# Output blocks of one tile by seven half-width products instead of eight, their operand sums on GpSimd

## The chip, the cores and the metric

One core of a Trainium2 chip runs the whole kernel. The metric is the device time of one execution in microseconds (us). TensorE (PE) multiplies matrices into PSUM banks; VectorE (DVE), ScalarE (ACT) and GpSimd (POOL) do element-wise work; SyncE (SP) issues the transfers (DMA). Each engine works through its own queue in order.

## The reference

A recurrent attention with a decay per head, then a feed-forward layer that multiplies two projections element by element:

```
for t in range(S):                                  # B, H, S, D = 4, 8, 768, 64
    state = gamma * state + k[:, :, t] (outer) v[:, :, t]
    y[:, :, t] = scale * q[:, :, t] @ state
x = y as (B*S, H*D) = (3072, 512)
a = x @ w_a;  b = x @ w_b                           # d_ff = 1536
return (a * b @ w_out)                              # (3072, 512), float32
```

## The kernel before

The 3072 tokens are 24 slots of 128. Seven tiles take them in turn: `TILES = [4, 2, 2, 2, 2, 4, 8]` (line 16), so tile 0 is slots 0 to 3, tile 1 is slots 4 and 5, tile 2 slots 6 and 7. A program written out by hand (lines 887 to 1068) fixes the order of each engine's instructions: `seq` (line 94) chains every instruction behind the one before it on the same engine, and between engines only data and buffers make one wait.

Around the change the program does these things.

- `casts_two(t)` and `casts(t)` (lines 304 and 287) prepare slots: GpSimd scales k and q into `kqb` (line 280) and copies v into `vb` (line 239), SP issues the DMA transpose of `kqb` into `kqT` (`flip`, line 300) and then the loads of a later slot. All of this goes into the queues of GpSimd and SP at the place of the call.
- `turn(new, old)` (line 389) does the attention of a pair of slots: `update` (TensorE into the state bank `st`, then a cast to `gst` by ScalarE or by the engine given), `scores` (TensorE into two banks, then two DVE multiplications by the mask into `aT`, line 333) for the new pair; `inter`, `intra` (TensorE into the banks `y0`, `y1`) and `leave` (ScalarE) for the old pair.
- `ffn_ab(J, ft)` computes one of the 12 column blocks of a*b for tile J: four matmuls for a, a ScalarE copy, four for g, a DVE multiplication into `ht` (lines 522 to 536).
- `ffn_out(J, i, n)` (line 553) is half n of the plain output block i of tile J: six matmuls of 512 columns. Both halves make one block of 128 rows; ScalarE copies it out, and the store is put on SP's queue by the next `store()`.
- `Group(J, i, A, B, C)` (line 617) makes two output blocks at once in the Strassen-Winograd manner, by seven products `p1` to `p7` of six matmuls of 256 columns each, in three PSUM banks A, B and C. `p2` ends with a DVE addition that reads bank C, after which C goes back to the ring; `p7` takes bank B; `p4` and `p5` end with DVE additions that read bank B; `p1`, `p6`, `p5` are followed by ScalarE snapshots of bank A, `p3` by a ScalarE copy.
- The products need sums of operands. `weight_sum(3)`, `(2)`, `(1)`, `(4)` (line 576) make T3, T2, T1 and T4 out of the output weights, each in two DVE halves of 768 elements a partition; they are made once and used by every tile. `hsum(J, s, a, b, eng)` (line 596) makes sum s of tile J out of `ht`: sum 3 is read by `p7`, 2 by `p6`, 1 by `p5`, 4 by `p3`. `hsums` makes 2, 1 and 4. T3 is read by `p7`, T2 by `p6`, T1 by `p5`, T4 by `p4`.
- The ring `psff` (line 69) hands out the three banks `ff0` to `ff2` in the order in which they were given back. `hs_tile` (line 588) says out of which pool a tile's sums come: `wstage`, which has six buffers under the tag `w`, or `raw`.

In the version before, the four output blocks of tile 0 are all made by `ffn_out`, and tiles 1 and up use `Group`. The branch for tile 0 in `hs_tile` is not reached.

Of the kernel before, what the change touches and what calls it, by code (L numbers as in the profile page):

```python
# [10 lines left out]
BF16 = mybir.dt.bfloat16  # L11
# [12 lines left out]
def kernel(  # L24
# [11 lines left out]
    P = 128  # L36
# [19 lines left out]
    wstage = ctx.enter_context(tc.tile_pool(name="wstage", bufs=6))  # L56
    raw = ctx.enter_context(tc.tile_pool(name="raw", bufs=3))
    nat = ctx.enter_context(tc.tile_pool(name="nat", bufs=6))
    tra = ctx.enter_context(tc.tile_pool(name="tra", bufs=4))
# [45 lines left out]
    def load_slot(t, names="kqv"):  # L105
        b, ci = divmod(t, NCH)
        for nm in names:
            src = {"k": k, "q": q, "v": v}[nm]
            if nm == "q":
                if t % 2 == 0:  # L110
                    load_two(nm, src, b, ci // 2, t)
                continue
            if t % 2 == 0:
                whole[nm] = raw.tile([P, 2, H, D], F32, tag=nm + "f", name=nm + "f")
            raws[nm, t] = whole[nm][:, t % 2]
            s = src[b, :, ci * P : (ci + 1) * P, :].rearrange("h p d -> p h d")
            seq(nc.sync.dma_start(out=raws[nm, t], in_=s))
# [108 lines left out]
    NP = NFT // 2  # L226
# [5 lines left out]
    BIG = len(TILES) - 1  # L232
    NS = NP - 1

    def cast(engine, dst, src):
        if engine is nc.scalar:
            seq(nc.scalar.copy(dst, src))
        else:
            seq(engine.tensor_copy(dst, src))  # L239
# [19 lines left out]
    kb, qb, vb, kqT, aT = {}, {}, {}, {}, {}  # L259
# [9 lines left out]
    def scaled(eng, t, i):  # L269
        tab = tabs[0] if i else tabs[1 if t < 2 * PAIRS else 2]  # L270
        dst, src, tab = kqb[t][:, i], raws["kq"[i], t], tab[:, t % NCH]
        if t < 2 * PAIRS:
            dst, src = (x.rearrange("p (hp r) d -> p hp r d", r=2) if x is src else x
                        for x in (dst, src))
            tab = tab.rearrange("p (hp r) o -> p hp r o", r=2).to_broadcast([P, HP, 2, D])
        else:
            dst = dst.rearrange("p hp r d -> p r hp d")
            src = src.rearrange("p (r hp) d -> p r hp d", r=2)
            tab = tab.rearrange("p (r hp) o -> p r hp o", r=2).to_broadcast([P, 2, HP, D])
        seq(eng.tensor_tensor(dst, src, tab, op=ALU.mult))  # L280

    def new_nat(t):
        kqb[t] = nat.tile([P, 2, HP, 2, D], BF16, tag="kqb", name="kqb")
        kb[t], qb[t] = kqb[t][:, 0], kqb[t][:, 1]
        vb[t] = nat.tile([P, H, D], BF16, tag="vb", name="vb")

    def casts(t):
        new_nat(t)
        scaled(nc.gpsimd, t, 0)
        scaled(nc.gpsimd, t, 1)  # L290
        if t not in range(12, 20):
            cast(nc.gpsimd, vb[t], raws["v", t])
        flip(t)
        if t + 2 < NSLOT:
            load_slot(t + 2)

    def flip(t):
        if t % 2 == 0:
            kqT[t // 2] = tra.tile([P, 2, 2, HP, P], BF16, tag="kqT", name="kqT", bufs=3)
        seq(nc.sync.dma_start_transpose(  # L300
            out=kqT[t // 2][:, t % 2].rearrange("p a b c -> p (a b) c"),
            in_=kqb[t].rearrange("p a hp r d -> p (a hp r d)")))
# [67 lines left out]
    def intra(t):  # L370
        for r in range(2):
            for j in range(2):
                for c in range(2):
                    hp = 2 * j + c
                    seq(nc.tensor.matmul(ys[t // 2][r][half(c), j, :, t % 2, :],  # L375
                                         vb[t][:, HP * r + hp, :], aT[t][:, r, hp, :],
                                         start=begin(t, c, r), stop=True, skip_group_check=True))
# [11 lines left out]
    def turn(new, old, eng=nc.scalar):  # L389
        if old is not None:  # L390
            ys[old // 2] = [psat.tile([P, 2, 2, 2, P // 2], F32, tag=f"y{r}", name="y") for r in range(2)]
        two = new is not None and (new + 1) % NCH < NCH - 1
        if new is not None:
            if two or old is None:
                update(new, eng)
            scores(new + 1, "y" if old is None else "ff")
            scores(new, "at")
        if old is not None:
            inter(old)
            inter(old + 1)  # L400
        if two:
            update(new + 1, nc.scalar)
        elif new is not None and old is not None:
            update(new, eng)
        if old is not None:
            intra(old)
            intra(old + 1)
            leave(old)
# [144 lines left out]
    def ffn_out(J, i, n):  # L553
        if n == 0:
            store()
            plain_out[i] = psff.tile([P, DM], F32, tag="ff", name="o")
        o = plain_out[i]
        for ft in range(NP * n, NP * n + NP):
            seq(nc.tensor.matmul(o, ht[J][:, ft, i * P : (i + 1) * P], wo_bf[:, ft],  # L559
                                 start=(ft == 0), stop=(ft == NFT - 1), skip_group_check=True))  # L560
        if n:
            osb = osbp.tile([P, DM], F32, tag="osb", name="osb")
            cast(nc.scalar, osb, o)
            psff.back(o)
            held.append((rows(J, i // 2, i % 2), osb))
# [5 lines left out]
    def tt(dst, x, y, op, eng=nc.vector):  # L571
        seq(eng.tensor_tensor(dst, x, y, op=op))  # L572
# [3 lines left out]
    def weight_sum(n, halves=(0, 1)):  # L576
        if n == 1 and not T1:
            T1.append(wstage.tile([P, NP, DH], BF16, tag="w", name="wsum1"))
        x, y, op = {3: (B22, B12, ALU.subtract), 2: (T3, B11, ALU.add), 4: (B21, T2, ALU.subtract),
                    1: (B12, B11, ALU.subtract)}[n]  # L580
        dst = T1[0] if n == 1 else {2: T2, 3: T3, 4: T4}[n]
        for i in halves:
            j = slice(NP // 2 * i, NP // 2 * (i + 1))
            tt(dst[:, j], x[:, j], y[:, j], op)

    hs = {}

    def hs_tile(J, s):
        if (J, s) not in hs:
            pool, tag = (raw, ("kf", "qf", "vf", "kf")[s - 1]) if J in (0, (BIG, 1)) else (wstage, "w")  # L590
            bufs = {}
            if (J, s) == (0, 4):
                pool, tag, bufs = tra, "kqT", {"bufs": 3}
            hs[J, s] = pool.tile([P, NP, 2, P], BF16, tag=tag, name=f"hs{s}", **bufs)

    def hsum(J, s, a, b, eng=nc.vector):
        U = slice(int(J == 0), 2 if isinstance(J, tuple) else TILES[J] // 2)
        hs_tile(J, s)
        v = ht[J].rearrange("p (k j) (u r n) -> p r k j u n", k=2, r=2, n=P)
        A11, A12, A21, A22 = (v[:, r, k2, a:b, U] for r in range(2) for k2 in range(2))  # L600
        S = {x: hs[J, x][:, a:b, U] for x in (1, 2, 3, 4) if (J, x) in hs}
        x, y, op = {3: (A11, A21, ALU.subtract), 2: (A22, S[3], ALU.subtract), 1: (A21, A22, ALU.add),
                    4: (A12, S.get(2), ALU.subtract)}[s]
        tt(S[s], x, y, op, eng)

    def hsums(J, a, b, eng):
        for s in (2, 1, 4):
            hsum(J, s, a, b, eng)
# [94 lines left out]
    FF = (psff, "ff")  # L703
# [3 lines left out]
    def single(J, A, B, C):  # L707
        g = Group(J, 0, A, B, C)
        g.p1()
        g.p7()  # L710
        g.p2()
        ffn_ab(J + 1, 0)
        g.p6()
        ffn_ab(J + 1, 1)
        g.p5()
        ffn_ab(J + 1, 2)
        g.p3()
        g.p4()
# [166 lines left out]
    D_, G_, A_ = nc.vector, nc.gpsimd, nc.scalar  # L885
# [72 lines left out]
    V_ = nc.vector  # L958
# [7 lines left out]
    def three(J, ft):  # L966
        store()
        for f in range(ft, ft + 3):
            ffn_a(J, f)
        for f in range(ft, ft + 3):  # L970
            ffn_g(J, f)
# [4 lines left out]
    for ft in range(NFT):  # L976
        ffn_ab(1, ft)
    casts_two(6)
    ffn_out(0, 0, 0)
    weight_sum(3)  # L980
    weight_sum(2)
    ffn_out(0, 0, 1)
    weight_sum(1)
    ffn_out(0, 1, 0)
    ffn_out(0, 1, 1)
    weight_sum(4)
    casts(8)
    ffn_out(0, 2, 0)
    ffn_out(0, 2, 1)
    turn(6, None, V_)  # L990
    hsum(1, 3, 0, 6)
    hsums(1, 0, 6, V_)
    ffn_out(0, 3, 0)
    ffn_out(0, 3, 1)
    casts(9)
    turn(None, 6)
    single(1, AT0, AT1, FF)
    casts(10)
    casts(11)
# [1 line left out]
    hsum(2, 3, 0, 6, G_)  # L1001
    blocks(2, 6, 7)
    turn(8, None)
    three(2, 7)
    hsums(2, 0, 3, G_)
    casts(12)
    turn(None, 8)
    blocks(2, 10, NFT)
    hsums(2, 3, 6, G_)
# [3 lines left out]
    blocks(3, 3, 4)  # L1013
    turn(10, None, V_)
    three(3, 4)
    hsum(3, 3, 0, 6, G_)
    v_cast(12)
    blocks(3, 7, 8)
    v_cast(13)
    blocks(3, 8, 9)  # L1020
    casts(15)
    hsums(3, 0, 3, G_)
    blocks(3, 9, 10)
    turn(12, 10)
# [74 lines left out]
```

## Time and profile before

| | us |
|---|---|
| time, median of three runs | 221.23 |
| the three runs | 220.83, 221.27, 221.23 |
| the profiled execution's own time | 221.23 |
| its span in the trace | 219.5 |
| TensorE busy / GpSimd busy / DVE busy | 212.4 / 142.1 / 139.1 |

The span is counted from the first instruction to the last; 1.7 us of the time lie around it. Times in a row of the timeline are the start, counted from the start of the span, and the length. In square brackets stands the idle time of the engine before the row and what ended it. Rows merge like instructions that follow one another (x36), so a length can be that of several.

### The profile page before, as it was taken

To read this page: it belongs to the slowest core of one execution; us is meant where nothing else is said; L and a number is where in the kernel's file an instruction comes from. 1 tells how busy PE (TensorE), PEld (TensorE's weight loads), DVE (VectorE), ACT (ScalarE), POOL (GpSimd) and SP (SyncE) were. 2 spreads that over 40 slices of the span, in tenths; PEclk is the share of its full clock that TensorE was granted. 3 is DMA by queue.
4 is the path that set the end of the run, shared out by engine and by line. 5 is a ranking of instruction groups with operands and counts; after the bars stand their busy time and mean duration, and the time that the engine had idled before them with its cause. 6 is when DMAs were issued, how large, how long until landed. Compare 5 with 4: busy or idle time off the path is not lost.

```text
span 219.5 us, 5638 instructions
## 1 busy us (share of the span) xinstructions
PE 212.4 (97%) x2242; PEld 143.6 (65%) x2242; DVE 139.1 (63%) x254; ACT 99.3 (45%) x217; POOL 142.1 (65%) x163
## 2 busy tenths in 40 slices
PE   7789999999999999999999999999999999999994
PEld 3457445687458888888888655456865444448883
DVE  3776346846783463675477246986595787789642
ACT  3256325343234453455576345445545656642331
POOL 5266876778444659669675958999999975520000
PEclk9999999999999999999999999999999999999999
DMA  6999999999999995999999999960022000000055
GB/s 168 290 323 367 384 315 358 379 244 247 221 243 232 275 201 131 217 191 281 174 220 239 218 170 227 266 61 3 4 85 106 0 1 3 0 0 1 27 191 167
DMA packets 85146, 39.68 MB, mean 181 GB/s; under 512 B 57472, under 2 KB 78848, under 8 KB 85120
## 3 DMA queue, kind: packets, MB, share of 16 engines
q1 hardware_dynamic: 84976, 39.26, 76.4%
q8 instruction: 17, 0.28, 0.6%
q10 hardware_dynamic: 144, 0.07, 0.1%
q14 instruction: 9, 0.07, 0.1%
HBM read 28.31 MB, written 6.29 MB: 158 GB/s over the span
## 4 chain that ended last, share of the span: by engine, by line
PE 89%; SPq 3%; DMA 3%; issue 1%; DVE 1%; POOL 0%; ACT 0%; DVEq 0%
PE a L522 19%; PE g L534 19%; PE mA L638 12%; PE uA L778 8%; PE mB L638 6%; PE o L559 5%; PE uB L778 4%; SPq L126 3%; DMA wsta<-in_moe_w_a_dram 3%; PE mC L638 3%; PE at L327 2%; PE uC L778 2%; PE y L375 2%; PE ka L837 2%; PE kb L837 2%; PE st L345 1%
## 5 line engine op out<-in xcount | busy, mean ns | idle before, releaser
L536 DVE TENSOR_TENSOR ht<-g,asb 128x256 bf16<-128x256 f32 (+1 forms) x74 | 36.9, 502 | 37.0 <-PE g L534 32.3
L522 PE MATMUL a<-xt,wa_bf 128*128 128x256 bf16 (+1 forms) x296 | 52.4, 304 | 0.4 <-DVE ht L536 0.2
L534 PE MATMUL g<-xt,wb_bf 128*128 128x256 bf16 (+1 forms) x296 | 52.2, 304 | 0.0
L525 ACT CAST asb<-a 128x256 bf16<-128x256 f32 (+1 forms) x74 | 32.4, 437 | 39.2 <-PE a L522 37.1
L534 PEld LDWEIGHTS <-wb_bf 128*128 128x128 bf16 x296 | 28.6, 98 | 12.6
L522 PEld LDWEIGHTS <-wa_bf 128*128 128x128 bf16 x296 | 27.9, 98 | 13.0 <-DVE xt L239 0.7
L280 POOL TENSOR_TENSOR kqb<-kf,ktab 128x512 bf16<-128x512 f32 x22 | 23.1, 1056 | 16.3 <-DMA kf<-in_k_dram 10.7
L638 PEld LDWEIGHTS <-hs 128*128 128x128 bf16 x240 | 23.3, 98 | 3.9
L333 DVE TENSOR_TENSOR aT<-at,mask 128x512 bf16<-128x512 f32 x36 | 22.3, 681 | 0.3
L784 ACT COPY snap<-uA 128x512 f32<-128x512 f32 x30 | 16.7, 588 | 12.6 <-PE uA L778 12.6
L280 POOL TENSOR_TENSOR kqb<-qf,qtab 128x512 bf16<-128x512 f32 x18 | 19.3, 1071 | 3.0 <-DMA qf<-in_q_dram 3.0
L645 ACT COPY snaps<-mA 128x256 f32<-128x256 f32 x30 | 11.2, 374 | 19.8 <-PE mA L638 19.7
L572 POOL TENSOR_TENSOR hs<-ht,hs 128x384 bf16<-128x384 bf16 (+1 forms) x17 | 16.6, 983 | 5.3 <-DVE ht L536 5.3
L638 PEld LDWEIGHTS <-ht 128*128 128x128 bf16 x180 | 17.5, 98 | 2.8
L572 POOL TENSOR_TENSOR ht<-gsb,asb 128x512 bf16<-128x512 bf16 x12 | 13.6, 1158 | 6.3 <-DVE gsb L572 6.3
L572 POOL TENSOR_TENSOR hs<-ht 128x384 bf16<-128x384 bf16 (+2 forms) x12 | 13.8, 1153 | 4.2 <-DVE ht L536 4.2
L638 PE MATMUL mA<-wsum,hs 128*128 128x256 bf16 x120 | 15.7, 273 | 0.0
L239 POOL CAST vb<-vf 128x512 bf16<-128x512 f32 x16 | 10.3, 657 | 7.5 <-DMA vf<-in_v_dram 7.0
L572 DVE TENSOR_TENSOR osb<-mB,snaps 128x256 f32<-128x256 f32 x20 | 8.4, 422 | 9.1 <-PE mB L638 4.7
L386 ACT CAST xt<-y 128x512 bf16<-128x512 f32 x18 | 9.7, 589 | 2.3 <-PE y L375 2.2
L559 PE MATMUL o<-wo_bf,ht 128*128 128x512 bf16 x48 | 10.7, 379 | 0.0
L572 DVE TENSOR_TENSOR gsb<-uB,snap 128x512 bf16<-128x512 f32 x10 | 6.9, 686 | 4.2 <-ACT snap L784 2.6
(104 smaller groups left out, 327.2 us busy)
## 6 DMA issues: line engine op xcount, KB each, us to landing
qf<-in_q_dram SPq DMA_DIRECT2D x12, 512.0 KB, 5.7
out_dram<-osb SPq DMA_DIRECT2D x21, 256.0 KB, 4.1
kf<-in_k_dram SPq DMA_DIRECT2D x18, 256.0 KB, 4.3
vf<-in_v_dram SPq DMA_DIRECT2D x18, 256.0 KB, 5.2
wsta<-in_moe_w_a_dram SPq DMA_DIRECT2D x6, 512.0 KB, 7.7
wstb<-in_moe_w_b_dram SPq DMA_DIRECT2D x6, 512.0 KB, 8.0
wsto<-in_moe_w_out_dram SPq DMA_DIRECT2D x6, 512.0 KB, 8.9
kf<-in_k_dram SPq DMA_DIRECT2D x3, 512.0 KB, 7.1
```

Of the source, the lines that this page charges most:

```text
L280: seq(eng.tensor_tensor(dst, src, tab, op=ALU.mult))
L333: seq(nc.vector.tensor_tensor(aT[t][:, r], at[r], mask.to_broadcast([P, HP, P]), op=ALU.mult))
L522: seq(nc.tensor.matmul(a, wa_bf[:, kt, fs], xcols(J, kt, c0, c1), start=(kt == 0), stop=(kt == KT - 1)))
L525: seq(nc.scalar.copy(asb, a))
L534: seq(nc.tensor.matmul(g, wb_bf[:, kt, fs], xcols(J, kt, c0, c1), start=(kt == 0), stop=(kt == KT - 1)))
L536: seq(nc.vector.tensor_tensor(ht[J][:, ft, c0:c1], g, asbs.pop((J, ft, c0)), op=ALU.mult))
L559: seq(nc.tensor.matmul(o, ht[J][:, ft, i * P : (i + 1) * P], wo_bf[:, ft], start=(ft == 0), stop=(ft == NFT - 1), skip_group_check=True))
L572: seq(eng.tensor_tensor(dst, x, y, op=op))
L638: seq(nc.tensor.matmul(m, w, right[:, j], start=(first and j == 0), stop=(j == NP - 1), skip_group_check=True))
L645: seq(nc.scalar.copy(self.snaps[:, n], self.bank["A"]))
L778: seq(nc.tensor.matmul(m, w, right[:, k], start=(first and k == 0), stop=(k == 1), skip_group_check=True))
L784: seq(nc.scalar.copy(self.snaps[n], self.bank["A"]))
```

## The change

Blocks 0 and 1 of tile 0 stay plain. Blocks 2 and 3 become one `Group(0, 1, FF, FF, FF)`, all three banks out of the ring. Its four operand sums are put on GpSimd, behind the preparation of slots 6 and 7 and so ahead of `casts(8)`. The parts of the group, the two plain blocks, the weight sums and `turn(6, None)` are put in a new order; the state cast in that turn goes to ScalarE. `hsums(1, ...)` moves behind `p4`. The sums of tile 0 now come out of `wstage`. Further on, `casts(12)` is called ahead of `three(2, 7)` and `hsums(2, 0, 3)`, and `casts(15)` ahead of `hsum(3, 3)`.

```diff
@@ -587,11 +587,8 @@
     def hs_tile(J, s):
         if (J, s) not in hs:
-            pool, tag = (raw, ("kf", "qf", "vf", "kf")[s - 1]) if J in (0, (BIG, 1)) else (wstage, "w")
-            bufs = {}
-            if (J, s) == (0, 4):
-                pool, tag, bufs = tra, "kqT", {"bufs": 3}
-            hs[J, s] = pool.tile([P, NP, 2, P], BF16, tag=tag, name=f"hs{s}", **bufs)
+            pool, tag = (raw, ("kf", "qf", "vf", "kf")[s - 1]) if J == (BIG, 1) else (wstage, "w")
+            hs[J, s] = pool.tile([P, NP, 2, P], BF16, tag=tag, name=f"hs{s}")
@@ -976,24 +973,30 @@
     for ft in range(NFT):
         ffn_ab(1, ft)
     casts_two(6)
-    ffn_out(0, 0, 0)
+    hsum(0, 3, 0, 6, G_)
+    hsums(0, 0, 6, G_)
+    g = Group(0, 1, FF, FF, FF)
     weight_sum(3)
     weight_sum(2)
+    ffn_out(0, 0, 0)
     ffn_out(0, 0, 1)
     weight_sum(1)
+    casts(8)
+    g.p1()
+    g.p2()
+    weight_sum(4)
     ffn_out(0, 1, 0)
+    turn(6, None)
+    g.p7()
+    g.p6()
     ffn_out(0, 1, 1)
-    weight_sum(4)
-    casts(8)
-    ffn_out(0, 2, 0)
-    ffn_out(0, 2, 1)
-    turn(6, None, V_)
+    g.p5()
     hsum(1, 3, 0, 6)
-    hsums(1, 0, 6, V_)
-    ffn_out(0, 3, 0)
-    ffn_out(0, 3, 1)
     casts(9)
     turn(None, 6)
+    g.p3()
+    g.p4()
+    hsums(1, 0, 6, V_)
     single(1, AT0, AT1, FF)
     casts(10)
     casts(11)
@@ -1001,9 +1004,9 @@
     hsum(2, 3, 0, 6, G_)
     blocks(2, 6, 7)
     turn(8, None)
+    casts(12)
     three(2, 7)
     hsums(2, 0, 3, G_)
-    casts(12)
     turn(None, 8)
@@ -1013,12 +1016,12 @@
     turn(10, None, V_)
     three(3, 4)
+    casts(15)
     hsum(3, 3, 0, 6, G_)
     v_cast(12)
     blocks(3, 7, 8)
     v_cast(13)
     blocks(3, 8, 9)
-    casts(15)
     hsums(3, 0, 3, G_)
```

## The prediction

> **What bounds the kernel now.** I read the busy times first, then TensorE's own waits and the windows, and then the timeline of each engine around the change.
>
> ```profile
> span 219.5 us, 5638 instructions
> PE 212.4 (97%) x2242; PEld 143.6 (65%) x2242; DVE 139.1 (63%) x254; ACT 99.3 (45%) x217; POOL 142.1 (65%) x163
> ...
> PE idle L506 <- DVE zero L173: 1.5, 1, 1.5
> ...
> 50.00:100.00 50.00, 49.91 (x617) 38.35 (x616) 30.65 (x63) 20.69 (x51) 31.92 (x34) 1.00 1.07 218
> 52.96:65.41 12.45, 12.45 (x122) 6.04 (x120) 9.94 (x17) 2.86 (x7) 5.72 (x7) 1.00 1.17 240
> ```
>
> TensorE is busy for 212.4 of 219.5 us, its longest wait is 1.5 us at the very start, and in the window of the change (52.96 to 65.41) it is busy for all of the 12.45 us at a granted clock of 1.00. So a us less of matmuls is a us less of time, and a us in which TensorE stands still is a us more. In the same window DVE is at work for 9.94 of 12.45 us: this engine is the next in line here, although its share of the whole span is only 63%.
>
> ```profile
> 52.96 7.93 PE L559 MATMUL o<-wo_bf,ht 128*128 128x512 bf16 x36
> 60.83 0.32 PE L345 MATMUL st<-vb,kqb 128*64 128x64 bf16 x8
> ...
> 61.91 2.76 PE L559 MATMUL o<-wo_bf,ht 128*128 128x512 bf16 x12
> 64.60 0.31 PE L365 MATMUL y<-kqT,gst 64*64 64x128 bf16 x8
> 64.84 0.64 PE L375 MATMUL y<-aT,vb 128*64 128x128 bf16 x16
> 65.41 0.83 PE L638 MATMUL mA<-wo_bf,ht 128*128 128x256 bf16 x6
> 66.08 0.82 PE L638 MATMUL mB<-wsum,hs 128*128 128x256 bf16 x6
> ...
> 76.21 0.32 PE L345 MATMUL st<-vb,kqb 128*64 128x64 bf16 x8
> ```
>
> The reader is to see the spacing of starts, since lengths overlap. 36 plain matmuls take 60.83 - 52.96 = 7.87 us, so a half block of six takes 1.31. A product of six at 256 columns takes 66.08 - 65.41 = 0.66 (0.67 by these two rows, rounded; half of 1.31 is 0.655). The new half of `turn(6)` takes 61.91 - 60.83 = 1.08, the old half 0.81.
>
> **What the products save.** Two plain blocks are four half blocks, 4 x 1.31 = 5.25 us. Seven products are 7 x 0.655 = 4.59. The gain in matmuls is 0.66 us, and it is all that the change can gain here. If nothing waited, tile 1's first product would start at 65.41 - 0.66 = 64.75 instead of 65.41.
>
> **What the sums cost.** DVE does the weight sums in this stretch, and GpSimd works beside it:
>
> ```profile
> 53.58 0.87 DVE L572 TENSOR_TENSOR wsum<-wo_bf 128x768 bf16<-128x768 bf16 x1
> 54.37 0.55 DVE L572 TENSOR_TENSOR wsum<-wo_bf 128x768 bf16<-128x768 bf16 x1
> 54.83 0.55 DVE L572 TENSOR_TENSOR wsum<-wsum,wo_bf 128x768 bf16<-128x768 bf16 x1
> 55.30 1.39 DVE L572 TENSOR_TENSOR wsum<-wsum,wo_bf 128x768 bf16<-128x768 bf16 x1
> 56.62 0.96 DVE L572 TENSOR_TENSOR wsum<-wo_bf 128x768 bf16<-128x768 bf16 x1
> 57.50 0.55 DVE L572 TENSOR_TENSOR wsum<-wo_bf 128x768 bf16<-128x768 bf16 x1
> ...
> 61.53 2.48 DVE L333 TENSOR_TENSOR aT<-at,mask 128x512 bf16<-128x512 f32 x4
> ```
>
> ```profile
> 52.41 0.62 POOL L239 CAST vb<-vf 128x512 bf16<-128x512 f32 x1
> 52.99 1.04 POOL L280 TENSOR_TENSOR kqb<-kf,ktab 128x512 bf16<-128x512 f32 x1
> 55.11 1.17 POOL L280 TENSOR_TENSOR kqb<-qf,qtab 128x512 bf16<-128x512 f32 x1 [1.08 <-DMA qf<-in_q_dram]
> 56.23 0.94 POOL L239 CAST vb<-vf 128x512 bf16<-128x512 f32 x1
> 59.96 1.04 POOL L280 TENSOR_TENSOR kqb<-kf,ktab 128x512 bf16<-128x512 f32 x1 [2.79 <-DMA kf<-in_k_dram]
> ...
> 76.08 1.64 POOL L572 TENSOR_TENSOR hs<-ht 128x768 bf16<-128x768 bf16 x1 [1.72 <-DVE ht L536]
> ```
>
> One DVE half sum takes 0.55 us when GpSimd is idle (57.50), and 0.87, 1.39 and 0.96 when a GpSimd instruction is running as it starts. The 1.39 one is the clearest: it starts at 55.30, GpSimd scales q from 55.11 to 56.28, and it ends at 56.69, about 0.4 after that. Next the copy of v takes 0.94 instead of 0.62: it starts at 56.23 and loses 0.32 behind that half sum. So the two do not share; one stands until the other is done. Later in the trace both have long queues of such work at once:
>
> ```profile
> 156.22 1.32 DVE L572 TENSOR_TENSOR xs<-xt 128x1024 bf16<-128x1024 bf16 x1 [3.79 <-ACT xt L386]
> 157.06 1.48 POOL L572 TENSOR_TENSOR wsb<-wb_bf,wsb 128x512 bf16<-128x512 bf16 x1
> 157.62 1.47 DVE L572 TENSOR_TENSOR xs<-xs,xt 128x1024 bf16<-128x1024 bf16 x1
> 158.50 1.60 POOL L572 TENSOR_TENSOR wsa<-wa_bf 128x512 bf16<-128x512 bf16 x1
> 159.01 1.64 DVE L572 TENSOR_TENSOR xs<-xt 128x1024 bf16<-128x1024 bf16 x1
> 160.06 1.60 POOL L572 TENSOR_TENSOR wsb<-wb_bf 128x512 bf16<-128x512 bf16 x1
> ...
> L572 POOL TENSOR_TENSOR hs<-ht,hs 128x512 bf16<-128x512 bf16 x5 | 5.7, 1150 | 0.0
> ```
>
> GpSimd's starts are 1.44 and 1.56 us apart where one such instruction takes 1.15 undisturbed, and in every such period DVE gets one instruction through, never two: strict turns, DVE holding for about 0.3 to 0.4 us.
>
> In the new order GpSimd is free at 52.99 (the copy of v for slot 7 ends) and has seven instructions without a break: four tile sums at 1.64 (row 76.08, the same shape), then k, q and v of slot 8 at 1.04, 1.04 and 0.62. DVE has six half sums ahead of `p2`'s addition, the first ready at 53.58, behind a tile sum that already runs. A turn is 1.64 + 0.33 = 1.97, back to back a little less; I take 1.93, since rows that follow one another overlap by some 0.04. GpSimd's first sum ends at 54.6, DVE's first half sum at 54.9; the second and third at 56.85 and 58.8; the fourth, behind the last tile sum, at 60.7; the fifth and sixth, behind k and q, at 62.05 and 63.4. `p2`'s addition reads PSUM and one SBUF operand and takes 0.42 (row below); it ends at about 63.9.
>
> ```profile
> 67.66 0.42 DVE L572 TENSOR_TENSOR osb<-mC,snaps 128x256 f32<-128x256 f32 x1 [1.65 <-PE mC L638]
> ```
>
> **Where TensorE meets it.** At its own pace TensorE runs block 0 (2.62), `p1` and `p2` (1.31), half of block 1 (1.31) and the new half of `turn(6)` (1.08) and stands before `p7` at 52.96 + 6.32 = 59.3. The ring gives: block 0 one bank, back; A the second, C the third, back after `p2`; block 1 the first; so `p7`'s B is C's bank and waits for the addition. It starts at about 63.95: a stall of 4.65 us. Were B another bank, `p6` would wait for T2 (60.7), `p5` for T1 (63.4), and the end would still come from the masks: DVE's queue behind the addition is two half sums of T4 (behind v of slot 8 and k of slot 9, whose load is there at 59.96), to about 65.6, then the four mask multiplications, 2.48, to 68.1. TensorE, from 63.95: `p7`, `p6`, half block, `p5`, 3.28, to 67.2, `inter(7)` to 67.5, and `intra` needs the last mask at 68.1. From there 12 of the 16 matmuls of the 0.57 us remain (0.43), then `p3` and `p4` (1.31): tile 1's first product starts at about 69.95. Against 65.41 that is +4.5 us, the 0.66 gained being in it. `hsums(1)`, now behind `p4`'s addition, meets slot 10's scaling on GpSimd; its last sum and the addition of bank C behind it come near the ring's next use. Bounds: 0, or one more GpSimd instruction of 1.04; I take 0.2, because two blocks of `ffn_ab` lie between. Sum on the profiled execution: 221.23 + 4.5 + 0.2 = 225.9; it equals the median of the runs.
>
> The stall's size hangs on how long DVE holds its turn. The Trainium skill, "SBUF — State Buffer", section "Who interferes with whom", has the first to issue hold the shared pair of ports for its whole instruction, a two-input SBUF `tensor_tensor` against GpSimd's reads among them. By that with the 0.55 of an undisturbed half sum each of six turns would be 0.2 longer and the time 227.1; the 0.32 that the copy of v loses is nearer to what the traces bear out.
>
> **The other edits.** Slot 8's scaling now ends near 63.1 instead of 57.2, and SP's queue holds its transpose, the loads of slot 10 and everything behind until then.
>
> ```profile
> 58.63 1.30 SPq L300 DMA_TRANSPOSE kqT<-kqb  x1
> ...
> 65.77 1.62 SPq L300 DMA_TRANSPOSE kqT<-kqb  x1
> ...
> kqT<-kqb SPq DMA_TRANSPOSE x18, 4.9
> ```
>
> Slot 9's transpose slips from 65.77 to some 68, and lands 4.9 us later, at 73. `turn(8)` reads it at 76.21, or 80.7 in the new run: cover of over 3 us even without a delay of TensorE, so nothing. The state cast on ScalarE costs nothing, ScalarE being busy for 2.86 of the 12.45 us. `casts(12)` and `casts(15)`:
>
> ```profile
> 80.37 0.92 POOL L572 TENSOR_TENSOR hs<-ht,hs 128x384 bf16<-128x384 bf16 x1 [2.64 <-DVE ht L536]
> ...
> 96.91 1.05 POOL L280 TENSOR_TENSOR kqb<-kf,ktab 128x512 bf16<-128x512 f32 x1 [0.23 <-DMA kf<-in_k_dram]
> 101.62 0.82 PE L638 MATMUL mB<-wsum,hs 128*128 128x256 bf16 x6
> ```
>
> Before the sums of tile 2 GpSimd waits 2.64 us for DVE; slot 12's two scalings (2 x 1.04) fit in. Slot 15's k waits for its load to 96.9; with both scalings ahead of it, sum 3 of tile 3 ends at 96.9 + 2.1 + 1.64 = 100.6, a us before `p7` reads it at 101.62. Both cost nothing; should slot 15's load be late by more than that us, the excess is lost, up to about 1 us. With TensorE 4.5 us later both have more room.
>
> **The rivals.**
> 1. *The two engines pass each other.* If tile sums on GpSimd and weight sums on DVE ran side by side, the weight sums would end by 58 as now, the addition at 58.5, ahead of 59.3; only the 0.66 would count: 220.6. For it: undisturbed half sums follow one another every 0.46 us (54.37 to 54.83), and six of them fit ahead of 59.3. Against it: the rows at 55.30 and 156 to 160.
> 2. *DVE gets two through per turn.* Then six half sums need three turns, the addition ends near 60.3, the masks near 64.7 instead of 68.1: 3.4 less, 222.5. Against it: between 156 and 160 it never does.
> 3. *TensorE's clock falls in the pause.* If after standing still for 4.65 us it ran at half rate through the 4.5 us behind, up to 4 us would be lost, of which the wait for the masks already covers 0.6; with half of that stretch affected, about +1.7: 227.6. The rows have no pause over 1.5 us, and the clock is 1.00 throughout, so they cannot decide it. The Trainium skill, "TensorE: Matmul & The Clock Gate", Part 1, says the clock halves after an idle window of about 3.4 us that runs freely and returns after as long a busy one; a pause of 4.65 us holds such a whole window in about a third of the phases, an estimate from that page. No run here shows it yet.
> 4. *The saving is not there*: the half-width matmuls of the ring's banks run slower than 0.655 a product. Against it: tile 1's products at 65.41. Worth 0.66 at most, to either of the others.
>
> **How the numbers follow.** The forecast has 0.60 with 224.5 to 227.1 as its own range (the turn between 1.8 and 2.2 us, the end of the chain with it); rival 3 has 0.17, rival 2 has 0.12, rival 1 has 0.11 (0.10 of it faster, 0.01 eaten up by rival 4). Range: 222.3 to 228.4, which leaves out rival 1 and the longest form of rival 3. A difference under 0.2%, 0.44 us, cannot be told from no change. Faster 0.10 (rival 1, -0.6), same 0.02, slower 0.88.
>
> **What would show it.** In the changed trace: DVE's `wsum` rows of 1.5 to 2 us between 53 and 63 with one GpSimd `hs` row between each two; TensorE idle for 4 to 5 us before `mB` (line 638), released by DVE's `osb<-mC`; the masks at 65 to 68; tile 1's first product near 70; and from there on everything later by one amount. It would be wrong if the `wsum` rows stayed at 0.55 or if `mB` of the new group followed the scores without a gap; a granted clock under 1.00 after the pause would be rival 3.

## The result, and the profile after

| | before | after |
|---|---|---|
| median, us (six runs each) | 221.09 | 227.19 |
| all runs | 220.83 to 221.27 | 226.36 to 227.81 |
| ratio, 95% interval | | 1.0276 (1.0257 to 1.0294) |
| profiled execution: time / span, us | 221.23 / 219.5 | 227.74 / 226.0 |

The changed kernel is 2.8% slower. TensorE's timeline of the changed kernel, in the same columns as before:

```profile
59.22 0.32 PE L345 MATMUL st<-vb,kqb 128*64 128x64 bf16 x8
63.93 1.44 PE L635 MATMUL mB<-wsum,hs 128*128 128x256 bf16 x6 [4.39 <-DVE osb L572]
65.16 1.49 PE L635 MATMUL mA<-wsum,hs 128*128 128x256 bf16 x6
66.44 2.77 PE L559 MATMUL o<-wo_bf,ht 128*128 128x512 bf16 x6
69.00 1.13 PE L635 MATMUL mA<-wsum,hs 128*128 128x256 bf16 x6
70.06 0.31 PE L365 MATMUL y<-kqT,gst 64*64 64x128 bf16 x8
...
72.19 0.82 PE L635 MATMUL mA<-wo_bf,ht 128*128 128x256 bf16 x6
```

There are two things to see. TensorE stands still for 4.39 us before `p7`, released by DVE's addition. And behind the pause the same work takes twice its time: `p7` takes 65.16 - 63.93 = 1.23 us where tile 1's first product took 0.67, the half block 2.56 where it took 1.31. Tile 1's first product starts at 72.19 in place of 65.41. The windows of the changed kernel give the cause (in each row the stretch, each engine's busy time with its count of instructions, then the granted clock, the DMA share and GB/s):

```profile
60.00:62.00 2.00, 0.00 (x0) 0.00 (x0) 2.00 (x2) 0.00 (x0) 2.00 (x3) 1.00 0.31 64
62.00:64.00 2.00, 0.07 (x1) 0.07 (x1) 2.00 (x4) 0.00 (x0) 2.00 (x3) 0.70 0.00 0
64.00:66.00 2.00, 2.00 (x10) 1.40 (x10) 2.00 (x3) 0.00 (x0) 2.00 (x3) 0.50 0.74 135
66.00:68.00 2.00, 2.00 (x8) 0.91 (x6) 2.00 (x4) 0.37 (x1) 1.19 (x2) 0.50 0.91 229
68.00:70.00 2.00, 2.00 (x9) 0.96 (x7) 0.13 (x1) 0.59 (x1) 1.04 (x1) 0.59 1.17 288
70.00:72.00 2.00, 2.00 (x37) 1.65 (x36) 1.29 (x2) 1.51 (x4) 1.59 (x2) 1.00 1.16 245
```

The granted clock falls to 0.50 within the pause, stays there until just before 70, and is back at 1.00 from then on. In the first two windows TensorE has nothing to do, while DVE and GpSimd are busy for 2.00 of 2.00 us. What they do is in the two timelines of the changed kernel, DVE first:

```profile
53.47 3.62 DVE L572 TENSOR_TENSOR wsum<-wo_bf 128x768 bf16<-128x768 bf16 x2
57.02 3.89 DVE L572 TENSOR_TENSOR wsum<-wsum,wo_bf 128x768 bf16<-128x768 bf16 x2
60.83 2.71 DVE L572 TENSOR_TENSOR wsum<-wo_bf 128x768 bf16<-128x768 bf16 x2
63.46 0.41 DVE L572 TENSOR_TENSOR osb<-mC,snaps 128x256 f32<-128x256 f32 x1
63.80 1.94 DVE L572 TENSOR_TENSOR wsum<-wo_bf,wsum 128x768 bf16<-128x768 bf16 x2
65.66 2.47 DVE L333 TENSOR_TENSOR aT<-at,mask 128x512 bf16<-128x512 f32 x4
```

```profile
53.13 1.64 POOL L572 TENSOR_TENSOR hs<-ht 128x768 bf16<-128x768 bf16 x1
54.85 1.83 POOL L572 TENSOR_TENSOR hs<-ht,hs 128x768 bf16<-128x768 bf16 x1
56.64 1.95 POOL L572 TENSOR_TENSOR hs<-ht 128x768 bf16<-128x768 bf16 x1
58.55 1.95 POOL L572 TENSOR_TENSOR hs<-ht,hs 128x768 bf16<-128x768 bf16 x1
60.45 1.36 POOL L280 TENSOR_TENSOR kqb<-kf,ktab 128x512 bf16<-128x512 f32 x1
```

A DVE row marked x2 holds two half sums; taken one by one, the first five start at 53.47, 55.10, 57.02, 58.93 and 60.83, each behind the start of one GpSimd instruction. A half sum takes 1.71 to 1.99 us beside a tile sum and 1.39 beside a scaling; before it was 0.55 to 1.39. GpSimd's first sum takes 1.64, the last two 1.95, 0.31 longer: that is what DVE holds in its turn. The addition and the masks (one SBUF operand beside PSUM) are as fast as ever, 0.41 and 2.47 us.

### The profile page after: what moved, and what is told of

It is laid out like the page before. It is cut to its first block, busy times and chain, and to the rows that moved or that the text cites. A ratio compares the mean times of both kernels' runs of the same rounds, so it can differ in the third digit from the quotient of the medians.

```text
span 226.0 us, 5682 instructions
## 1 busy us (share of the span) xinstructions
PE 214.3 (95%) x2260; PEld 146.6 (65%) x2260; DVE 146.4 (65%) x256; ACT 100.0 (44%) x220; POOL 150.2 (66%) x167
## 4 chain that ended last, share of the span: by engine, by line
PE 85%; DVE 4%; SPq 4%; DMA 4%; issue 1%; POOL 0%; ACT 0%; DVEq 0%
PE a L522 19%; PE g L534 19%; PE mA L635 13%; PE uA L775 8%; PE mB L635 7%; PE uB L775 4%; DVE wsum L572 4%; DMA wstb<-in_moe_w_b_dram 4%; SPq L126 3%; PE mC L635 3%; PE at L327 2%; PE y L375 2%; PE uC L775 2%; PE ka L834 2%; PE kb L834 2%; PE st L345 1%
## 5 line engine op out<-in xcount | busy, mean ns | idle before, releaser
L635 PEld LDWEIGHTS <-hs 128*128 128x128 bf16 x264 | 26.4, 101 | 9.7 <-issue 4.9
L280 POOL TENSOR_TENSOR kqb<-kf,ktab 128x512 bf16<-128x512 f32 x22 | 23.8, 1085 | 12.0 <-DMA kf<-in_k_dram 11.7
L642 ACT COPY snaps<-mA 128x256 f32<-128x256 f32 x33 | 12.3, 373 | 27.9 <-PE mA L635 27.7
L572 POOL TENSOR_TENSOR hs<-ht 128x384 bf16<-128x384 bf16 (+2 forms) x14 | 17.4, 1245 | 9.2 <-DVE ht L536 9.2
L572 POOL TENSOR_TENSOR hs<-ht,hs 128x384 bf16<-128x384 bf16 (+2 forms) x19 | 20.4, 1079 | 4.5 <-DVE ht L536 4.3
L635 PEld LDWEIGHTS <-ht 128*128 128x128 bf16 x198 | 19.4, 98 | 3.2
L635 PE MATMUL mA<-wsum,hs 128*128 128x256 bf16 x132 | 18.3, 282 | 0.0
L572 DVE TENSOR_TENSOR osb<-mB,snaps 128x256 f32<-128x256 f32 x22 | 9.2, 422 | 12.2 <-ACT snaps L642 6.8
L635 PE MATMUL mB<-wsum,hs 128*128 128x256 bf16 x66 | 9.5, 285 | 4.4 <-DVE osb L572 4.4
L237 ACT CAST gst<-st 128x256 bf16<-128x256 f32 x14 | 5.2, 372 | 10.0 <-PE st L345 10.0
```

The source lines that it names most:

```text
L635: seq(nc.tensor.matmul(m, w, right[:, j], start=(first and j == 0), stop=(j == NP - 1), skip_group_check=True))
L642: seq(nc.scalar.copy(self.snaps[:, n], self.bank["A"]))
```

## The experiments

Theory: DVE's weight sums and GpSimd's tile sums take strict turns, one instruction each; DVE's addition and masks behind them come late; TensorE stands still; and the clock falls in the pause and makes it dearer. The rivals are named with each run. Every time stands beside runs of the kernel before on the same chip, 220.96 to 221.01 us in the median; an interval that does not reach 1 is a difference.

**The tile sums left out (e1).**

```diff
-    hsum(0, 3, 0, 6, G_)
-    hsums(0, 0, 6, G_)
     g = Group(0, 1, FF, FF, FF)
...
-                    w = hs[J, left][:, j, self.n]
+                    w = hs[J, left][:, j, self.n] if J != 0 else ht[0][:, NP + j, 2 * P : 3 * P]
```

> The four GpSimd sums of tile 0 are left out; the products p7, p6, p5, p3 of the new group read ht itself, so the second half of tile 0's output is another. Theory of turns: without the four sums GpSimd meets DVE only with slot 8's scaling, as before the change; the fifth and sixth half sums end near 58, p2's addition near 58.4, ahead of p7 at 59.2; no pause, no fall of the clock, and the 0.66 us of seven products for eight remain: 220.4 us. Rival (the group and the new order of TensorE cost time by themselves, whatever the sums do): 222 us or more, with waits left in TensorE's queue. Rival (the pause comes from the ring bank alone): a pause of some length before p7 stays, 223 us or more.

Measured: 220.56 us, ratio 0.9981 (0.9973 to 0.9989). Its TensorE timeline:

```profile
59.28 0.83 PE L635 MATMUL mB<-wsum,ht 128*128 128x256 bf16 x6
...
64.77 0.82 PE L635 MATMUL mA<-wo_bf,ht 128*128 128x256 bf16 x6
```

`p7` follows at its own pace, and tile 1's first product is 0.64 us earlier than before the change. Its products of tile 0 read `ht` in place of the sums, so half of that tile's output is another; their number, size and order are those of the changed kernel. The seven products and the new order cost nothing; the whole loss comes with the four sums.

**The sums alone, with no group (e7).** The kernel before, with the two `hsum` calls of the change put behind `casts_two(6)` and their buffers taken out of `wstage`, as in the changed kernel.

> The kernel before with the four GpSimd sums of tile 0 put behind slots 6 and 7 and read by nobody; no group, no new order. Theory of turns: DVE's eight half sums take one GpSimd instruction each, the sixth ends near 63.4, the state cast and the masks of turn(6) follow to about 68; TensorE, done with its plain blocks at 63.4, waits 4 to 5 us for them; 224 to 226 us, with a clock at half for some us if the pause is long. Rival (the loss comes from the group's products and their order): 221.2 us, as before.

Measured: 227.62 us, 1.0301 (1.0285 to 1.0317). The theory's numbers were too low; the mechanism is in its TensorE timeline:

```profile
60.92 0.64 PE L327 MATMUL at<-kqT 64*64 64x128 bf16 x32
65.98 0.43 PE L345 MATMUL st<-vb,kqb 128*64 128x64 bf16 x8 [4.41 <-DVE gst L239]
```

Sums that nobody reads cost as much as the whole change, by the wait for another DVE instruction, the state cast, which stands behind the weight sums in the old order. I had the wait begin at 63.4; it begins at 61.6, since here DVE makes the state cast that the second `update` waits for. The granted clock falls to 0.50 here too.

**The bank wait alone taken away (e3).**

```diff
     weight_sum(3)
-    weight_sum(2)
...
-    weight_sum(1)
     casts(8)
     g.p1()
     g.p2()
+    weight_sum(2)
+    weight_sum(1)
     weight_sum(4)
```

> DVE does only T3 ahead of p2's addition; T2, T1, T4 come behind it. Theory of turns: the addition ends near 57.2, p7 starts at 59.5 with no pause, but DVE's queue is as long as before: p6 waits for T2 to about 61, p5 for T1 to about 63.8, intra for the last mask to about 68.1; tile 1's first product near 69.9, 225.6 us, or up to 2 us more if the clock falls in the last of these waits (3.6 us). Rival (the ring bank of p7 is the whole cause): no pause left, 220.5 to 221.5 us.

Measured: 227.56 us, 1.0298 (1.0274 to 1.0322). Its TensorE timeline:

```profile
59.35 0.83 PE L635 MATMUL mB<-wsum,hs 128*128 128x256 bf16 x6
...
66.46 0.21 PE L365 MATMUL y<-kqT,gst 64*64 64x128 bf16 x1 [2.31 <-DVE aT L333]
...
69.04 1.46 PE L635 MATMUL mA<-wo_bf,hs 128*128 128x256 bf16 x6
```

`p7` starts at 59.35 without a pause, and nothing is won: two waits of 0.5 us for T2 and T1, then 2.31 for the masks. The rival falls. The ring bank only decides where TensorE meets DVE's late queue. The clock also falls here (`p3` at 69.04 has a length of 1.46 us in place of 0.82), though no single wait is longer than 2.31 us.

**The pause filled (e2).**

```diff
+    zw = const.tile([P, P], BF16, name="zw")
+    seq(nc.gpsimd.memset(zw, 0.0))
...
     turn(6, None)
+    for _ in range(18):
+        seq(nc.tensor.matmul(plain_out[1], zw, wo_bf[:, 0], start=False, stop=False,
+                             skip_group_check=True))
     g.p7()
```

> The changed kernel with 18 matmuls of 512 columns by a block of zeros between turn(6) and p7, added into the open bank of block 1, so that TensorE has 3.9 us of work in the pause of 4.4 us. Theory (pause plus fall of the clock): p7 starts at the same place, 63.7 to 63.9, the granted clock stays at 1.00, the masks at 68.1 become what intra waits for, and tile 1's first product starts near 69.9 instead of 72.2: 225.3 us. Rival (the fall of the clock is hidden behind the wait for the masks anyway): 227 us as the changed kernel. Rival (the matmuls themselves run past p7's release): over 227 us.

Measured: 226.15 us, 1.0237 (1.0222 to 1.0251); the changed kernel's own interval is 1.0257 to 1.0294. Its TensorE timeline:

```profile
63.80 0.81 PE L637 MATMUL mB<-wsum,hs 128*128 128x256 bf16 x6 [0.48 <-DVE osb L574]
...
68.06 0.53 PE L377 MATMUL y<-aT,vb 128*64 128x128 bf16 x12 [0.29 <-DVE aT L335]
...
69.84 0.82 PE L637 MATMUL mA<-wo_bf,ht 128*128 128x256 bf16 x6
```

`p7` starts where it did, now at full pace; then the masks become the wait, as expected, and tile 1's first product is at 69.84 in place of 72.19: 2.35 us by the trace are the clock's part. In the medians it is 1.04. Two things lie between. The six runs of the changed kernel are not alike: four have a mean granted clock of 0.984 or 0.985, which is some 7 us at half rate over the span, and two have 0.991, some 4 us; these two are its shortest (226.36, 226.57). So the clock's part varies from run to run. And the filled kernel's four runs lie 0.3 to 1.4 us above the 225.3 expected; in its profiled run (226.35) the last product starts at 219.78 in a span of 224.5, 4.7 us before the end, where the kernel before has 4.1. Why the end is longer there stays open. (That run's mean clock is 0.997; up to 222.9 it is 1.00, and the half rate lies behind the last product.)

**The length and the number of the turns (e8, e9).** Once GpSimd's sums are cut in two, once DVE's halves are joined.

```diff
-    hsum(0, 3, 0, 6, G_)
-    hsums(0, 0, 6, G_)
+    for s in (3, 2, 1, 4):
+        hsum(0, s, 0, 3, G_)
+        hsum(0, s, 3, 6, G_)
```

> The changed kernel with each of GpSimd's four sums of tile 0 in two instructions of 384 elements (0.87 us apart where undisturbed) in place of one of 768; the same elements in all. Theory of turns: a DVE half sum waits for one GpSimd instruction whatever its length, so a turn shrinks from 1.93 to about 1.2 us: the sixth half sum ends near 60.3, p2's addition near 60.7, p7 starts there (a pause of 1.4 us), the last mask near 65.1, tile 1's first product near 66.9; both pauses too short for the clock to fall: 222.7 us. Rival (the two engines share a port's bandwidth, so the elements count and not the instructions): p7 near 63.9 and 227 us as the changed kernel.

```diff
-        for i in halves:
-            j = slice(NP // 2 * i, NP // 2 * (i + 1))
-            tt(dst[:, j], x[:, j], y[:, j], op)
+        tt(dst, x, y, op)
```

> The changed kernel with each weight sum as one DVE instruction of 1536 elements in place of two of 768. Theory of turns: four turns in place of eight; the third sum (T1) ends near 60.2, the addition near 60.6, the last mask near 65.1, tile 1's first product near 66.9; no fall of the clock: 222.7 us. Rival (the elements count): no change from the changed kernel, 227 us.

Measured: 224.23 (1.0142, 1.0126 to 1.0158) and 223.75 (1.0131, 1.0114 to 1.0147), both 3 us faster than the changed kernel with the same elements on each engine. The rival of a shared bandwidth falls. DVE's timeline of e8, then TensorE's:

```profile
53.42 2.07 DVE L572 TENSOR_TENSOR wsum<-wo_bf 128x768 bf16<-128x768 bf16 x2
55.42 2.45 DVE L572 TENSOR_TENSOR wsum<-wsum,wo_bf 128x768 bf16<-128x768 bf16 x2
```

```profile
60.62 0.82 PE L635 MATMUL mB<-wsum,hs 128*128 128x256 bf16 x6 [1.39 <-DVE osb L572]
...
66.83 0.82 PE L635 MATMUL mA<-wo_bf,ht 128*128 128x256 bf16 x6
...
89.06 0.50 PE L635 MATMUL mA<-wsum,hs 128*128 128x256 bf16 x3 [1.52 <-POOL hs L572]
```

A pair of half sums takes 2.45 us in place of 3.89 (one turn is now about 1.2), `p7` waits 1.39, tile 1's first product is at 66.83 (66.9 expected). But both times are over the 222.7 expected, and the last row shows where: 22 us later TensorE waits 1.52 us for a GpSimd sum of tile 2 (1.12 at the same place in e9). GpSimd's timeline of e8 ahead of it:

```profile
82.39 1.04 POOL L280 TENSOR_TENSOR kqb<-kf,ktab 128x512 bf16<-128x512 f32 x1 [1.25 <-DMA kf<-in_k_dram]
84.50 1.04 POOL L280 TENSOR_TENSOR kqb<-qf,qtab 128x512 bf16<-128x512 f32 x1 [1.06 <-DMA qf<-in_q_dram]
85.50 0.91 POOL L572 TENSOR_TENSOR hs<-ht,hs 128x384 bf16<-128x384 bf16 x1
```

That is `casts(12)`, which the change put ahead of these sums: it waits for its loads, and the sums wait with it.

**The other two moves (e11, e4).** e11 is e8 with `casts(12)` and `casts(15)` back in their old places; e4 is the kernel before with nothing but their new ones.

> The kernel of e8 with casts(12) and casts(15) back in their old places. Theory: e8's wait of 1.52 us at 89.06 (p6 of tile 2, for GpSimd's sum) came from casts(12) standing ahead of the sums and waiting for its loads; with it behind them the wait goes and the time is 224.2 less 1.5, 222.7 us. Rival (GpSimd is late there for its own backlog, whatever stands ahead): 224 us as e8.

> The kernel before with nothing but casts(12) and casts(15) moved ahead. Prediction of record: nothing, 221.0 us within 0.44. Rival (k and q of slot 12 come from DMA after the sums of tile 2 could start, so that these are late for p6): 221.5 to 222.5 us, with a wait of TensorE for GpSimd near 86.

Measured: e11 222.86 us, 1.0081 (1.0068 to 1.0094), 1.4 less than e8, with no wait for a GpSimd sum: the theory was right. e4 221.10, 1.0007 (0.9995 to 1.0020): no difference. So the moves cost nothing in e4 and in the changed kernel, and 1.4 us in e8, where the load of slot 12's k comes late: it leaves SP's queue at 77.83, against 72.04 in e4 and 75.52 in the changed kernel, where the sums of tile 2 start 3.4 us later than in e8 (82.85 against 79.50). That slot 8's delay is what put this load back is not shown: in e6 below slot 8 comes first, and yet the load leaves at 74.54 and GpSimd waits 1.35 us for it.

**Slot 8 first (e5).**

```diff
     casts_two(6)
+    casts(8)
     hsum(0, 3, 0, 6, G_)
...
     weight_sum(1)
-    casts(8)
```

> The changed kernel with the scaling of slot 8 ahead of the four sums of tile 0 on GpSimd, as the order was before; nothing else moved. Theory of turns: the weight sums T3, T2, T1 run beside slot 8 as in the kernel before and end near 58.2, p2's addition at 58.6; the tile sums start near 58.1 and end at 59.7, 61.7, 63.6, 65.2 with T4's halves between; p7 waits 0.5 us, p6 1.3 us, the masks end near 64.5; tile 1's first product near 66.6 in place of 72.2: 222.3 us, clock at 1.00. Rival (the place ahead of slot 8 does not matter, since the sums meet DVE wherever they stand): 225 us or more.

Measured: 223.16 us, 1.0086 (1.0057 to 1.0115); four runs, two at 222.3 and 222.4 and two at 223.9 and 224.1. The place ahead of slot 8 is worth 4 us, the clock's part included (0.997 to 1.000 in these runs). The profiled run (224.10) has the first product of tile 1 at 67.73 where I expected 66.6, and behind it one wait that I had not counted, for the addition behind `hsums(1)`; its timeline has

```profile
71.89 0.60 PE L522 MATMUL a<-xt,wa_bf 128*128 128x256 bf16 x4 [0.50 <-DVE osb L572]
```

What parts the two pairs of runs stays open.

**A version that loses nothing (e6, e10, e12).** e6 puts slot 8 first, makes both plain blocks and the turn ahead of the group, and spreads T4:

```diff
         ffn_ab(1, ft)
     casts_two(6)
+    casts(8)
     hsum(0, 3, 0, 6, G_)
     hsums(0, 0, 6, G_)
...
     ffn_out(0, 0, 1)
     weight_sum(1)
-    casts(8)
+    ffn_out(0, 1, 0)
+    ffn_out(0, 1, 1)
+    turn(6, None)
     g.p1()
     g.p2()
-    weight_sum(4)
-    ffn_out(0, 1, 0)
-    turn(6, None)
+    weight_sum(4, (0,))
     g.p7()
     g.p6()
-    ffn_out(0, 1, 1)
-    g.p5()
-    hsum(1, 3, 0, 6)
     casts(9)
     turn(None, 6)
+    g.p5()
+    weight_sum(4, (1,))
+    hsum(1, 3, 0, 6)
+    s = Group(1, 0, AT0, AT1, FF)
+    s.p1()
+    s.p2()
     g.p3()
     g.p4()
     hsums(1, 0, 6, V_)
-    single(1, AT0, AT1, FF)
+    s.p7()
+    ffn_ab(2, 0)
+    s.p6()
+    ffn_ab(2, 1)
+    s.p5()
+    ffn_ab(2, 2)
+    s.p3()
+    s.p4()
     casts(10)
     casts(11)
```

> A new order of the same work: slot 8's scaling ahead of the tile sums; both plain blocks and turn(6) ahead of the group's first product; T4's halves behind the masks and behind p5's addition; tile 1's first two products ahead of p3 and p4. Theory of turns: the masks end near 61.4, each tile sum is there within 0.3 us of its product, T4 near 65.3; no pause of more than 0.3 us, clock at 1.00: the gain of 0.66 us less up to 0.3, 220.4 to 220.9 us. Rival (seven products with their sums do not fit beside slots 8 and 9 in any order): over 221.5 us.

e10 is e6 with `casts(12)` and `casts(15)` in their old places, e12 is e10 with whole weight sums as in e9 (T4 as one instruction at the first of its two places).

> The order of e6 with casts(12) and casts(15) back in their old places. Theory: the rest that e6 lost (222.3 against 220.4 to 220.9) is GpSimd's sums of tiles 2 and 3 standing behind scalings that wait for their loads (e6's profile has GpSimd wait 1.35 and 0.88 us for k and q of slot 12 right ahead of the sums of tile 2, and most of its runs are 1 us longer than the profiled one); with the scalings behind the sums again this goes: 220.4 to 220.8 us. Rival (the rest lies in the new order of the group itself): 222 us as e6.

> The order of e10 with the weight sums of e9, each one DVE instruction: four turns with GpSimd in place of eight, so that the masks no longer hang on whether slot 8's q arrives before or after a half sum. Theory of turns: the masks end near 61.4 in every execution, T4 and tile 1's sum 3 come a turn earlier than in e10, and the waits of 0.6 and 0.4 us in e10's profile shrink to under 0.3 together: 220.6 to 221.0 us, between the floor of e1 (220.56) and e10 (221.31). Rival (e10's rest is not DVE's turns but something else that comes with the tile sums): 221.3 us or more.

| | median, us | runs | ratio, 95% interval |
|---|---|---|---|
| e6 | 222.33 | 221.31 to 222.53 | 1.0054 (1.0037 to 1.0071) |
| e10 | 221.31 | 221.07 to 222.91 | 1.0023 (1.0007 to 1.0040) |
| e12 | 221.21 | 221.03 to 221.60 | 1.0008 (0.9999 to 1.0017) |

Each step took away what it was meant to (1.0 us by the old places of the scalings, then the spread of the runs), and e12 cannot be told from the kernel before; all three miss the gain expected. In e12's profile TensorE has no wait of 0.25 us or more in this stretch, but starts of its timeline lie further apart than the work between them:

```profile
58.18 0.32 PE L345 MATMUL st<-vb,kqb 128*64 128x64 bf16 x8
...
59.45 0.83 PE L633 MATMUL mA<-wo_bf,ht 128*128 128x256 bf16 x6
...
64.30 0.82 PE L633 MATMUL mC<-wo_bf,ht 128*128 128x256 bf16 x6
65.23 0.83 PE L633 MATMUL mA<-wo_bf,hs 128*128 128x256 bf16 x6
...
69.61 0.82 PE L633 MATMUL mA<-wsum,hs 128*128 128x256 bf16 x6
70.49 0.60 PE L522 MATMUL a<-xt,wa_bf 128*128 128x256 bf16 x4
```

The new half of the turn takes 1.27 us in place of 1.08, and the products at 64.30 and 69.61 0.93 and 0.88 in place of 0.66: 0.19 + 0.27 + 0.22 = 0.68, the gain of 0.66. That the order of e12 leaves just this much in small gaps is read from one profile.

## Why the prediction was right, point by point

- *TensorE is the bound, and seven products save 0.66 us.* Right: e1 has tile 1's first product 0.64 us earlier and is 0.41 us faster in the median.
- *Strict turns of 1.93 us, the addition at 63.9, `p7` at 63.95.* Right: GpSimd's sums start 1.91 and 1.90 us apart, the addition ends at 63.87, `p7` starts at 63.93. DVE's hold of 0.33 measured 0.31; the reading by an undisturbed instruction's full length, which gave 227.1, lands near the total by luck: the clock made up the rest, and the turns themselves speak against it. The first turns were shorter, 1.72 and 1.79. e8 and e9 show that it is the number of turns that sets DVE's delay: the same elements in shorter GpSimd pieces or in fewer DVE instructions cost 3 us less.
- *A stall of 4.65 us.* 4.39 of idle time, since TensorE came to `p7` at 59.5; it had already waited 0.2 us for slot 7's transpose.
- *The end of the chain is the last mask at 68.1, whichever bank `p7` takes.* The mask ended at 68.13, and e3 shows that another place of the bank wait changes nothing. The forecast has tile 1's first product at 69.95 by this path; its terms add up to 69.84 (68.1 + 0.43 + 1.31), and in e2, where the clock stayed, it starts at 69.84. In the changed kernel itself the masks did not decide: at half rate TensorE came to `intra` only at 70.
- *The clock.* This is the step of the forecast that failed. It kept the clock at 1.00 and had the fall as rival 3, at 0.17 and +1.7 us, 227.6. Rival 3 came true: the clock was at 0.50 from about 62.8 to 69.6, for 2.35 us by e2's trace, and the median is 227.19: above 227.1, the upper end of the forecast's own range, and inside the whole range only because that was made wide enough for rival 3. The rule that the forecast named from the Trainium skill, "TensorE: Matmul & The Clock Gate", Part 1 (half rate after an idle window of about 3.4 us, back after a busy one) fits in its length: the slow stretch is 6.83 us, two such windows. The estimate of a third of the phases was too low: the mean clocks of all six runs, 0.984 to 0.991, and those of e3 and e7, 0.983 to 0.992, are below those of every run of the kernel before on record (0.997 to 1.000). It counted only windows without any work, and the last section shows the clock falling after windows with some.
- *0.2 us for `hsums(1)` behind `p4`.* Not seen after 72.19 in the changed kernel. The wait exists: 0.50 us in e5.
- *The moves of `casts(12)` and `casts(15)` cost nothing.* Right in the changed kernel and by e4; the bound of about 1 us for a late load was set on slot 15, and it is slot 12 whose scaling cost 1.4 us in e8 (e11), once the pause was shorter.
- *Slot 8's delay costs nothing by itself.* Right in the changed kernel, where `turn(8)` came 6.8 us later; whether it is what made the load of slot 12 late in e8 is not shown (e6).

## What to carry to other kernels

Before a two-operand SBUF sum is given to GpSimd, count the two-operand SBUF sums of DVE that stand beside it: each waited here for one whole GpSimd instruction, so put short pieces on GpSimd and few long ones on DVE, or place the sums where DVE's queue holds PSUM reads. A stretch of 3.4 us in which TensorE works little, in one pause or in several, is priced with the clock, and a gain of 0.66 us is not worth an order in which one appears. A preparation moved ahead of work that TensorE needs carries the wait for its loads with it.

## What was not expected of the hardware

The clock fell in e3 although TensorE's longest single wait there was 2.31 us: the waits of 0.5, 2.3, 0.4 and 0.3 us lay close together, with a few small matmuls between. In e8 single waits of up to 1.52 us left it at 1.00. A pause is thus not safe just because no single wait reaches 3.4 us. The slow stretches point to another measure: they last 6.83, 3.41 and 6.83 us in the changed kernel, e3 and e7, one or two steps of 3.41. So here are the step ahead of the fall and those behind it, of the changed kernel, of e3, and last the emptiest 3.41 us of e8 between its start and its end (columns as in the windows above, TensorE's busy time first):

```profile
59.39:62.80 3.41, 0.15 (x8) 0.13 (x5) 3.41 (x3) 0.37 (x1) 3.41 (x3) 1.00 0.41 88
62.80:66.22 3.42, 2.29 (x11) 1.62 (x11) 3.42 (x5) 0.00 (x0) 3.42 (x4) 0.50 0.45 84
66.22:69.63 3.41, 3.41 (x11) 1.52 (x10) 1.91 (x4) 0.76 (x2) 1.95 (x3) 0.50 1.06 270
```

```profile
64.23:67.64 3.41, 0.52 (x8) 0.35 (x8) 3.41 (x6) 0.33 (x1) 3.03 (x3) 1.00 0.89 189
67.64:71.05 3.41, 3.22 (x26) 2.30 (x26) 2.17 (x3) 1.45 (x3) 1.81 (x2) 0.50 1.18 297
```

```profile
85.66:89.07 3.41, 1.89 (x19) 1.45 (x16) 0.85 (x2) 0.37 (x1) 3.41 (x5) 1.00 1.03 196
```

The clock fell after steps in which TensorE worked 0.15 us (changed kernel), 0.52 (e3) and 0.00 (e7), and stayed where it worked at least 1.89. At half rate, it stayed low after a step with 2.29 us of work and came back after one with 3.22 or 3.41. So by these rows it is the work within such a step that counts, not the longest wait; at the end of e10's trace it also fell after one with 1.20 (216.15 to 219.56), and between that and 1.89 these runs leave the limit open.
